# A retention-and-GLU kernel on one core: another order of first loads, split first gates, a ring of output rows, an earlier third pair

## The chip, the cores and the metric

The kernel runs on one core of a Trainium2 chip. A core has TensorE (PE, matrix products, with a separate weight-load step shown as PEld), VectorE (DVE), ScalarE (ACT), GpSimd (POOL) and SyncE (SP), each with its own instruction queue run in order, and 16 DMA engines that the queues feed. The metric is device time in microseconds, from the first to the last work of one execution. The kernel before took 339.49 us (median of six runs, 338.7 to 341.69).

## The reference

```python
scores = scale * np.matmul(q, k.transpose(0, 1, 3, 2))       # (8, 8, 576, 576), head size 64
gamma = 1.0 - 2.0 ** (-5.0 - np.arange(H))
Dmat = np.where(rel >= 0, gamma[:, None, None] ** rel, 0.0)    # rel = row - column
attn = np.matmul(scores * Dmat, v)                             # causal, decaying, no softmax
x = attn.transpose(0, 2, 1, 3).reshape(4608, 512)
gate = 1.0 / (1.0 + np.exp(-(x @ w_gate)))                     # 512 -> 1536
out = (gate * (x @ w_val)) @ w_out                             # 1536 -> 512, float32
```

Batch 8, 8 heads, 576 tokens, so 4608 rows for the gated layer. Inputs and output are float32; products run in bf16.

## The kernel before

**Retention by state.** The decay factors into a row factor on q and a column factor on k, so the first casts from float32 to bf16 multiply by small tables (L237 and L247/L257). Attention then needs only scores inside a chunk (masked), times v, plus q times a state: the running sum of k-transposed-v of all earlier chunks of that batch. The state sits in one PSUM bank (`st`), and each chunk copies it into a block-diagonal bf16 tile `sbd`, which the next chunk multiplies by its q. That is the state chain: state matmuls, copy, `inter` matmuls, next chunk.

**Three pairs, then 34 steps.** The first work is three "pairs" of two 128-token chunks each (batch 0 tokens 0-255 and 256-511, batch 1 tokens 0-255). A pair is cast (`cast_pair`, L234/L237), its k and q are transposed on PE (`turn`, L306, copied out by ACT at L316), scored (`pair_qk`, L325, masked by DVE at L330), multiplied by v (`pair_intra`, L365), joined with the state (`pair_st` L340, `tile_sv` L351, `pair_inter` L374) and written into `xT`, the transposed input of the gated layer (`pair_out`, L381/L384). All later chunks are "steps": POOL casts k, q and v (L247, L257, L268), a DMA transpose on SP turns them (`cross`, L284), and PE scores (L394), multiplies (L413, L415) and updates the state (L427).

**The gated layer.** `h` products take a 128-wide chunk of the 1536 (12 chunks) by a block of tokens: gate product, sigmoid on ACT, value product, multiplication on DVE into `gv`. `op` products (L557) multiply twelve `gv` by the out weights, 128 rows at a time; ACT copies the result into `ob` (L528) and SP stores it (L536). Tokens 0 to 511 come first and apart: gates in `h_both` (L606, sigmoid L610, product L613), out products in `op_first` (L733), with the third pair's work placed by hand between the out products. Then blocks of 256, 256, 4 x 384 and 4 x 512 tokens run through `h_units` (L490) and `op_units` (L557), and between their pieces the steps are advanced in proportion to the columns done.

**What sets the order.** The program's text: every engine runs its instructions in the order written, and semaphores between engines follow from which tile each one reads and writes. All loads, stores and DMA transposes but one store go through SP's queue, in the order written, and eight DMAs at most are under way. Loads use a ring of 18 buffers of 256 KB (`ld_pool`): pair 0, pair 1 (each k, q, k, q, v, v, by halves of the heads), gate and value weights, the twelve out weights, then pair 2, then steps. PSUM has eight banks: `tr`, two `qk`, `pv`, `st` and three `ffn`; a new tile of a name waits until the bank's last reader is done. `fill(n)` issues n matmuls of a blank tile that nobody reads, in places where PE would wait. Weight casts are dealt by hand to POOL, ACT and DVE. `store` holds each output row tile for two pieces of work before its DMA is written into SP's order (`tick`); rows of tokens before 768 wait until the block at 768.

## Time and profile before

| | |
|---|---|
| median of six runs | 339.49 us |
| the profiled execution | 338.84 us |
| its span, first to last instruction | 337.1 us |
| PE busy | 327.5 us (97%) |
| POOL, ACT, DVE busy | 185.4, 168.3, 163.6 us |
| DMA | 60.0 MB, 178 GB/s on average |
| first gate product of the gated layer | 19.65 us |
| first out product | 40.84 us |
| first product of the 512-token block (256 tokens) | 56.67 us |

The page of the profile is one execution. In the views by time a row has its start, how long it ran from its first start to its last end, engine, line, operation, output and input, how many instructions, and in brackets the engine's idle time ahead of it and what ended it. PE's matmuls overlap in the pipeline, so a row's length is a little more than the sum of the steps between starts. The granted clock of PE is 1.00 up to 331 us.

### The profile page before, as it was taken

What the parts mean: (1) busy time and instruction counts of PE and PEld (TensorE: products, weight loads), DVE (VectorE), ACT (ScalarE), POOL (GpSimd) and SP (SyncE); (2) the same over time, 40 slices, a digit from 0 to 9 for tenths busy, and PEclk for the clock granted to TensorE, in tenths of its full rate; (3) what the DMA queues carried; (4) which work ended last, traced back from release to release, by engine and by line L of the source; (5) the groups of instructions that cost most, each with busy time, mean ns of one, the idle gap of its engine ahead of it and who ended that gap; (6) DMA issues with size and microseconds to landing.
All of it is one profiled execution on the core that took longest, in us unless ns stands there. A gap on an engine that the chain in (4) does not pass through costs nothing.

```text
span 337.1 us, 7347 instructions
## 1 busy us (share of the span) xinstructions
PE 327.5 (97%) x2749; PEld 184.5 (55%) x2784; DVE 163.6 (49%) x327; ACT 168.3 (50%) x346; POOL 185.4 (55%) x327
## 2 busy tenths in 40 slices
PE   8899999999999999999999999999999999999996
PEld 4544445869666466556556655544555455444443
DVE  5744564726466455526446635642664156503320
ACT  6545535637665456355446655445545455233321
POOL 5574579788955979697548976482567500000000
PEclk9999999999999999999999999999999999999999
DMA  7999994899999999999969999892994440020002
GB/s 208 313 368 387 348 231 87 142 229 194 204 234 264 190 202 222 230 245 220 197 146 202 182 232 214 158 216 96 195 223 80 140 65 3 0 94 33 0 31 95
DMA packets 164100, 60.00 MB, mean 178 GB/s; under 512 B 144480, under 2 KB 156000, under 8 KB 164064
## 3 DMA queue, kind: packets, MB, share of 16 engines
q1 hardware_dynamic: 163920, 59.39, 85.5%
q8 instruction: 22, 0.36, 0.5%
q10 hardware_dynamic: 144, 0.13, 0.1%
q14 instruction: 14, 0.11, 0.1%
HBM read 37.75 MB, written 9.44 MB: 140 GB/s over the span
## 4 chain that ended last, share of the span: by engine, by line
PE 84%; DMA 7%; POOL 4%; issue 1%; DVE 1%; SPq 1%; ACT 0%; POOLq 0%; DVEq 0%
PE h L490 45%; PE op L557 23%; PE hg L606 3%; DMA T<-qk_nat 3%; PE hv L606 3%; PE qk L394 2%; PE pv L415 2%; DMA k32p<-in_k_dram 2%; PE pv L413 2%; DMA v32p<-in_v_dram 2%; PE st L427 2%; POOL qk_nat L247 1%; SPq L114 1%; PE op L547 1%; POOL qk_nat L257 1%
## 5 line engine op out<-in xcount | busy, mean ns | idle before, releaser
L490 PE MATMUL h<-xT,wg_sb 128*128 128x384 bf16 (+2 forms) x476 | 102.4, 336 | 0.4 <-DVE gv L518 0.2
L490 PE MATMUL h<-xT,wv_sb 128*128 128x384 bf16 (+2 forms) x473 | 102.2, 336 | 0.4
L247 POOL TENSOR_TENSOR qk_nat<-k,ktab 64x256 bf16<-64x256 f32 x120 | 73.5, 612 | 47.4 <-PE st L427 25.0
L518 DVE TENSOR_TENSOR gv<-g,h 128x384 bf16<-128x384 bf16 (+1 forms) x96 | 59.7, 622 | 71.7 <-PE h L490 56.7
L557 PE MATMUL op<-wo_sb,gv 128*128 128x512 bf16 x356 | 84.5, 379 | 0.8
L514 ACT ACTIVATE g<-h 128x384 bf16<-128x384 f32 (+1 forms) x96 | 52.2, 544 | 64.9 <-PE h L490 58.3
L433 DVE CAST sbd<-st 64x256 bf16<-64x256 f32 x104 | 43.7, 420 | 45.1 <-PE st L427 42.9
L490 PEld LDWEIGHTS <-wg_sb 128*128 128x128 bf16 x480 | 43.7, 98 | 31.4 <-issue 0.4
L490 PEld LDWEIGHTS <-wv_sb 128*128 128x128 bf16 x480 | 44.1, 98 | 29.0 <-issue 0.4
L557 PEld LDWEIGHTS <-gv 128*128 128x128 bf16 x372 | 34.4, 98 | 36.3
L268 POOL CAST vbd<-v 64x256 bf16<-64x256 f32 x120 | 47.6, 397 | 10.6 <-PE pv L415 6.1
L278 ACT CAST vs<-v 64x256 bf16<-64x256 f32 x104 | 41.9, 403 | 1.6
L528 ACT COPY ob<-op 128x512 f32<-128x512 f32 x34 | 19.8, 586 | 45.4 <-PE op L557 39.4
L257 POOL TENSOR_TENSOR qk_nat<-q,qtab 128x512 bf16<-128x512 f32 (+1 forms) x34 | 35.4, 1042 | 2.6
L417 ACT CAST xT<-pv 128x512 bf16<-128x512 f32 (+1 forms) x34 | 18.2, 534 | 18.1 <-PE pv L415 18.0
L396 DVE TENSOR_TENSOR pt<-qk,tri 128x512 bf16<-128x512 f32 (+1 forms) x34 | 21.2, 625 | 6.5 <-PE qk L394 6.2
L415 PE MATMUL pv<-pt,vbd 128*128 128x64 bf16 x240 | 18.0, 193 | 0.0
L427 PEld LDWEIGHTS <-qk_nat 128*128 128x128 bf16 x208 | 13.2, 98 | 8.8
L413 PE MATMUL pv<-T,sbd 128*128 128x64 bf16 x216 | 17.1, 193 | 0.0
L415 PEld LDWEIGHTS <-vbd 128*128 128x128 bf16 x240 | 15.2, 98 | 3.5
L413 PEld LDWEIGHTS <-sbd 128*128 128x128 bf16 x216 | 15.1, 98 | 2.5
L506 DVE TENSOR_TENSOR gv<-g,h 128x256 bf16<-128x256 bf16 x24 | 10.0, 421 | 12.2 <-ACT g L504 11.8
(76 smaller groups left out, 232.0 us busy)
## 6 DMA issues: line engine op xcount, KB each, us to landing
out_dram<-ob SPq DMA_DIRECT2D x34, 256.0 KB, 2.4
v<-in_v_dram SPq DMA_DIRECT2D x26, 256.0 KB, 4.2
k<-in_k_dram SPq DMA_DIRECT2D x26, 256.0 KB, 4.5
q<-in_q_dram SPq DMA_DIRECT2D x26, 256.0 KB, 5.1
wg<-in_moe_w_gate_dram SPq DMA_DIRECT2D x12, 256.0 KB, 5.7
wv<-in_moe_w_val_dram SPq DMA_DIRECT2D x12, 256.0 KB, 5.4
wo<-in_moe_w_out_dram SPq DMA_DIRECT2D x12, 256.0 KB, 5.3
k32p<-in_k_dram SPq DMA_DIRECT2D x6, 256.0 KB, 5.5
```

Source lines behind the costliest of these rows:

```text
L247: nc.gpsimd.tensor_tensor(out=kn[half(hh), j, :, half(hh)], in0=k32[half(j), hh::2, :], in1=ktab[half(j), c, hh::2].unsqueeze(2).to_broadc ...
L257: nc.gpsimd.tensor_tensor(out=qs[0:n], in0=q32[0:n], in1=qtab[0:n, c, :].unsqueeze(2).to_broadcast([n, H, D]), op=ALU.mult)
L268: nc.gpsimd.tensor_copy(out=vb[half(hh), j, :, half(hh)], in_=v32[half(j), hh::2, :])
L278: nc.scalar.copy(out=natural["vs", s][half(hh), j], in_=loaded[s][0][half(j), hh::2, :])
L396: nc.vector.tensor_tensor(out=pt[:, :, 0:n].rearrange("p m (j t) -> p m j t", t=64), in0=qkp[:, :, 0:n].rearrange("p m (j t) -> p m j t", ...
L413: nc.tensor.matmul(pvp[:, m, half(j)], lhsT=before[:, m, :], rhs=qT[:, m, half(j)], start=True, stop=False)
L415: nc.tensor.matmul(pvp[:, m, half(j)], lhsT=vb[:, j, m, :], rhs=pt[:, m, half(j)], start=before is None, stop=True)
L433: nc.vector.tensor_copy(out=sb[half(hh), :, half(hh)], in_=st_tiles[b][half(hh)])
L490: nc.tensor.matmul(out, lhsT=w_sb[:, kc, fc * P:(fc + 1) * P], rhs=xT[:, kc, t0 + a:t0 + e], start=(kc == 0), stop=(kc == NKC - 1))
L514: nc.scalar.activation(out=g[:, 0:n], in_=h1[:, 0:n], func=AF.Sigmoid)
L518: nc.vector.tensor_tensor(out=gvs[some[0]][:, a:e], in0=g[:, 0:n], in1=h2[:, 0:n], op=ALU.mult)
L557: nc.tensor.matmul(opp, lhsT=gvs[fc][:, nb * P:(nb + 1) * P], rhs=wo_sb[:, fc, :], start=(fc == 0), stop=(fc == NFC - 1))
```

## The change

Four edits, all in the order of work; nothing that is computed changes.

1. **Loads and the front.** k and q of pair 0 and pair 1 are loaded first (eight loads), then v of both (four). The front is written anew: casts of all k, then all v, then the first weights on POOL; scores of both pairs ahead of most v products; transposes in the banks `tr` and `pv`. Fillers go from 28 to 21, all into one tile.
2. **Gates of 256 tokens.** The first two chunks are computed by `h_half` on columns 0 to 255 and 256 to 511 apart, gate and value halves in one PSUM tile; the groups of columns 0 to 255 stand between the last state and `inter` steps of pair 1.
3. **The third pair.** Its k and q are loaded behind two out weights and its v behind six more; its transposes stand among the value products of chunks 8 to 11, its scores right behind them; two clears of `vbd` on POOL move ahead of the out weights.
4. **Ring of output rows.** A stored row tile's DMA is written when nine younger ones are held; the rest leave in the last two blocks.

```diff
             parts[nm, "pair", A, g] = t
+            yield
...
-    load_pair(0)
-    load_pair(1)
+    both = [load_pair(A) for A in range(2)]
+    for n_pair in (4, 2):
+        for one in both:
+            for _ in range(n_pair):
+                next(one)
     load_w(0, 2)
...
     load_w(8, 4)
-    for f in range(NFC):
-        load_wo(f)
-    load_pair(2)
+    pair_2 = load_pair(2)
+    for n_wo, n_pair in ((2, 4), (6, 2), (4, 0)):
+        for _ in range(n_wo):
+            load_wo(sum(1 for x in parts if x[0] == "o"))
+        for _ in range(n_pair):
+            next(pair_2)
     LEAD_CAST = 3
...
+    idle = ffn_psum.tile([P, 512], FP32, tag="ffn", name="idle")
     def fill(n):
...
-        ps = ffn_psum.tile([P, 512], FP32, tag="ffn", name=f"idle_{fill.at}")
-        fill.at += 1
         for i in range(n):
-            nc.tensor.matmul(ps, lhsT=blank[:, 0:P], rhs=blank, start=True, stop=True)
-    fill.at = 0
+            nc.tensor.matmul(idle, lhsT=blank[:, 0:P], rhs=blank, start=True, stop=True)
     fill(10)
...
         if g == 0:
-            probs["p", A] = att_pool.tile([P, 2, M, 2, P], BF16, tag="ptp", name=f"ptp_{A}", bufs=1)
+            probs["p", A] = att_pool.tile([P, 2, M, 2, P], BF16, tag="ptp", name=f"ptp_{A}", bufs=2)
         for hh in range(2):
...
+    def pair_tile(A, a, banks):
+        s = 2 * A + a
+        ps = [psum.tile([P, M // len(banks), P], FP32, tag=tag, name=f"pvp_{s}_{i}") for i, (psum, tag) in enumerate(banks)]
+        pair_ps[s] = [(ps[m * len(banks) // M], m % (M // len(banks)), M // len(banks)) for m in range(M)]
     def pair_intra(A, g, a):
         s = 2 * A + a
-        if g == 0:
-            pair_ps[s] = (tr_psum if a else pv_psum).tile([P, M, P], FP32, tag="tr" if a else "pv", name=f"pvp_{s}")
-        ps = pair_ps[s]
+        if s not in pair_ps:
+            pair_tile(A, a, [(tr_psum, "tr") if a else (pv_psum, "pv")])
         for i in range(2):
             m = 2 * g + i
+            ps, at_m, of = pair_ps[s][m]
             for r in range(2):
                 for hh in range(2):
-                    nc.tensor.matmul(ps[half(hh), m, :], lhsT=natural["v", A][half(a), r, 2 * m + hh, :],
+                    nc.tensor.matmul(ps[half(hh), at_m, :], lhsT=natural["v", A][half(a), r, 2 * m + hh, :],
                                      rhs=probs["p", A][half(a), hh, m, r, :],
-                                     start=(m == 0 and r == 0), stop=(m == M - 1 and r == 1),
+                                     start=(at_m == 0 and r == 0), stop=(at_m == of - 1 and r == 1),
                                      skip_group_check=True)
...
         for m in range(M):
-            nc.tensor.matmul(pair_ps[2 * A + a][:, m, :], lhsT=state[b, c - 1, 1][:, m, :],
+            ps, at_m, of = pair_ps[2 * A + a][m]
+            nc.tensor.matmul(ps[:, at_m, :], lhsT=state[b, c - 1, 1][:, m, :],
                              rhs=turned["qp", A][:, m, a * P:(a + 1) * P],
-                             start=False, stop=(m == M - 1), skip_group_check=True)
-    def pair_out(A, a, eng):
+                             start=False, stop=(at_m == of - 1), skip_group_check=True)
+    def pair_out(A, a, *engs):
         t0 = (2 * A + a) * P
-        if eng is not None:
-            eng(out=xT[:, :, t0:t0 + P], in_=pair_ps[2 * A + a])
-            return
-        for g, half_eng in enumerate((on_dve, on_act)):
-            half_eng(out=xT[:, 2 * g:2 * g + 2, t0:t0 + P], in_=pair_ps[2 * A + a][:, 2 * g:2 * g + 2])
+        k = M // len(engs)
+        for i, eng in enumerate(engs):
+            eng(out=xT[:, i * k:(i + 1) * k, t0:t0 + P], in_=pair_ps[2 * A + a][i * k][0])
...
-    LATE = 768
+    KEEP = 9
     stores = []
...
-    def store(opp, r0, hold, eng=None):
+    def leave():
+        r, ob = stores.pop(0)
+        for p0, r0, w in rows(r, P):
+            nc.sync.dma_start(out[r0:r0 + w, :], ob[p0:p0 + w])
+    def store(opp, r0, eng=None):
...
         (eng or on_act)(out=ob, in_=opp)
-        stores.append([hold if r0 >= LATE else 10 ** 6, r0, ob])
-    def tick(n=1):
-        for x in list(stores):
-            x[0] -= n
-            if x[0] <= 0:
-                for p0, r0, w in rows(x[1], P):
-                    nc.sync.dma_start(out[r0:r0 + w, :], x[2][p0:p0 + w])
-                stores.remove(x)
+        stores.append((r0, ob))
+        if len(stores) > KEEP:
+            leave()
...
                     yield 4 * 512
-            store(opp, t0 + nb * P, 2)
+            store(opp, t0 + nb * P)
             yield 4 * 512
...
         for _ in units:
-            tick()
+            pass
...
-    cast_pair("k", 0, 0, nc.gpsimd)
+    for A in range(2):
+        for g in range(2):
+            cast_pair("k", A, g, nc.gpsimd)
+    for A in range(2):
+        for g in range(2):
+            cast_pair("v", A, g, on_pool)
+    for i in range(2):
+        cast_w("g", 0, 2, i, on_pool)
+    for i in range(2):
+        cast_w("v", 0, 2, i, on_pool)
+    QK = [(qk_psum, "qk"), (qk_psum, "qk")]
+    FF = [(ffn_psum, "ffn"), (ffn_psum, "ffn")]
+    TR, PV = (tr_psum, "tr"), (pv_psum, "pv")
     cast_pair("q", 0, 0, nc.vector)
-    cast_pair("k", 0, 1, nc.gpsimd)
+    turn("k", 0, 0, *TR)
+    turn("q", 0, 0, *PV)
+    fill(3)
     cast_pair("q", 0, 1, nc.vector)
-    cast_pair("v", 0, 0, on_pool)
-    cast_pair("v", 0, 1, on_pool)
-    cast_pair("k", 1, 0, nc.gpsimd)
-    cast_pair("k", 1, 1, nc.gpsimd)
-    cast_pair("v", 1, 0, on_pool)
-    cast_pair("v", 1, 1, on_pool)
-    QK = [(qk_psum, "qk"), (qk_psum, "qk")]
-    turn("k", 0, 0)
-    turn("q", 0, 0)
-    fill(4)
-    turn("k", 0, 1)
     pair_qk(0, 0, QK)
-    turn("q", 0, 1)
+    turn("k", 0, 1, *TR)
+    fill(2)
+    turn("q", 0, 1, *PV)
     fill(3)
-    pair_qk(0, 1, QK)
+    cast_pair("q", 1, 0, nc.vector)
+    pair_qk(0, 1, FF)
+    turn("k", 1, 0, *TR)
+    turn("q", 1, 0, *PV)
+    fill(2)
+    cast_pair("q", 1, 1, nc.vector)
+    turn("k", 1, 1, *TR)
+    pair_qk(1, 0, QK)
+    fill(1)
+    turn("q", 1, 1)
     pair_intra(0, 0, 0)
...
     tile_sv(0, 0, (on_act, on_act))
-    cast_pair("q", 1, 0, nc.vector)
-    cast_pair("q", 1, 1, nc.vector)
-    fill(2)
-    turn("k", 1, 0)
     pair_intra(0, 1, 0)
+    pair_qk(1, 1, FF)
     pair_intra(0, 1, 1)
-    fill(2)
+    pair_st(0, 1)
     pair_inter(0, 1)
-    turn("q", 1, 0)
     pair_out(0, 0, on_act)
-    pair_st(0, 1)
-    fill(1)
-    turn("k", 1, 1)
     pair_out(0, 1, on_dve)
-    turn("q", 1, 1)
-    pair_qk(1, 0, QK)
     tile_sv(0, 1, (on_act, on_act))
-    fill(3)
-    pair_qk(1, 1, QK)
-    fill(1)
     pair_intra(1, 0, 0)
-    pair_inter(1, 0)
+    pair_tile(1, 1, QK)
     pair_intra(1, 0, 1)
+    pair_intra(1, 1, 0)
     pair_st(1, 0)
     tile_sv(1, 0, (on_act, on_act))
-    fill(2)
-    pair_intra(1, 1, 0)
-    pair_out(1, 0, on_act)
+    pair_inter(1, 0)
+    pair_out(1, 0, on_dve)
     pair_intra(1, 1, 1)
+    hp = {}
+    first_g = {}
+    def h_half(what, fc, x):
+        w_sb, i = (wg_sb, 0) if what == "g" else (wv_sb, 1)
+        if what == "g":
+            hp[fc, x] = ffn_psum.tile([P, 2, 256], FP32, tag="ffn", name=f"h_0_{x}_{fc}")
+        if x == 0 and what == "g":
+            first_g[fc] = g_pool.tile([P, 512], BF16, tag="g", name=f"g_0_{fc}")
+            gvs[fc] = gv_pool.tile([P, 512], BF16, tag="gv", name=f"gv_0_{fc}")
+        cols = slice(x * 256, x * 256 + 256)
+        for kc in range(NKC):
+            nc.tensor.matmul(hp[fc, x][:, i, :], lhsT=w_sb[:, kc, fc * P:(fc + 1) * P], rhs=xT[:, kc, cols],
+                             start=(kc == 0), stop=(kc == NKC - 1))
+        if what == "g":
+            nc.scalar.activation(out=first_g[fc][:, cols], in_=hp[fc, x][:, 0, :], func=AF.Sigmoid)
+        else:
+            nc.vector.tensor_tensor(out=gvs[fc][:, cols], in0=first_g[fc][:, cols], in1=hp[fc, x][:, 1, :], op=ALU.mult)
+    h_half("g", 0, 0)
     pair_inter(1, 1)
-    pair_out(1, 1, None)
-    for i in range(2):
-        cast_w("g", 0, 2, i, on_pool)
-    cast_w("v", 0, 2, 0, on_pool)
-    cast_w("v", 0, 2, 1, on_dve)
-    units = h_both((0, 1))
-    step(units, 1)
+    pair_out(1, 1, on_dve, on_act)
+    h_half("g", 1, 0)
     pair_st(1, 1)
     tile_sv(1, 1, (on_act, on_act))
-    step(units, 3)
+    h_half("v", 0, 0)
+    h_half("v", 1, 0)
+    for fc in range(2):
+        h_half("g", fc, 1)
+        h_half("v", fc, 1)
     for i in range(2):
...
     cast_w("v", 8, 4, 3, on_dve)
-    units = h_both((8, 9, 10, 11))
-    step(units, 2)
+    for t in vbd[0:2]:
+        nc.gpsimd.memset(t, 0.0)
     cast_wo(0, on_pool)
-    cast_wo(1, on_dve)
-    cast_wo(2, on_pool)
-    step(units, 2)
-    for f in range(3, 7):
-        cast_wo(f, on_pool if f % 2 else on_act)
-    step(units, 4)
-    for f in range(7, NFC):
-        cast_wo(f, on_pool if f % 2 else on_act)
     cast_pair("k", 2, 0, nc.gpsimd)
     cast_pair("k", 2, 1, nc.gpsimd)
+    cast_wo(1, on_dve)
+    cast_pair("q", 2, 0, nc.vector)
+    cast_pair("q", 2, 1, nc.vector)
+    units = h_both((8, 9, 10, 11))
+    step(units, 4)
+    cast_wo(2, on_pool)
+    turn("k", 2, 0, tr_psum, "tr")
+    step(units, 1)
+    cast_wo(3, on_act)
+    turn("q", 2, 0, pv_psum, "pv")
+    step(units, 1)
+    cast_wo(4, on_pool)
+    turn("k", 2, 1, tr_psum, "tr")
+    step(units, 1)
+    turn("q", 2, 1, pv_psum, "pv")
+    step(units, 1)
+    cast_wo(5, on_act)
+    cast_wo(6, on_pool)
+    cast_wo(7, on_pool)
     cast_pair("v", 2, 0, on_pool)
     cast_pair("v", 2, 1, on_pool)
-    cast_pair("q", 2, 0, nc.vector)
-    cast_pair("q", 2, 1, nc.vector)
-    nc.vector.memset(qk_nat[0], 0.0)
-    nc.vector.memset(qk_nat[1], 0.0)
-    later_constants()
-    for t in vbd[0:2]:
-        nc.gpsimd.memset(t, 0.0)
+    cast_wo(8, on_act)
+    cast_wo(9, on_pool)
+    cast_wo(10, on_act)
+    cast_wo(11, on_pool)
     loads_to(1)
...
     opps = [ffn_psum.tile([P, 512], FP32, tag="ffn", name=f"op_0_{nb}") for nb in range(3)]
-    op_first((0,), range(3), opps)
-    turn("k", 2, 0, tr_psum, "tr")
-    op_first((1,), range(3), opps)
-    turn("q", 2, 0, qk_psum, "qk")
-    op_first((2,), range(3), opps)
-    turn("k", 2, 1, pv_psum, "pv")
-    turn("q", 2, 1, qk_psum, "qk")
-    op_first((3, 4), range(3), opps)
     pair_qk(2, 0, QK)
-    op_first((5, 6), range(3), opps)
+    op_first((0, 1, 2), (0,), opps)
     pair_qk(2, 1, [(tr_psum, "tr"), (pv_psum, "pv")])
-    op_first((7,), range(3), opps)
+    nc.vector.memset(qk_nat[0], 0.0)
+    nc.vector.memset(qk_nat[1], 0.0)
+    op_first((0, 1, 2), (1, 2), opps)
+    later_constants()
+    op_first((3, 4, 5), range(3), opps)
     pair_st(2, 0)
     tile_sv(2, 0, (on_act, on_act))
-    cast_dense(0, 0)
-    cast_dense(0, 1)
-    op_first((8, 9, 10, 11), range(3), opps)
+    op_first((6,), range(3), opps)
     pair_intra(2, 0, 0)
...
     pair_out(2, 0, on_act)
-    store(opps[0], 0, 1, on_dve)
-    opps.append(ffn_psum.tile([P, 512], FP32, tag="ffn", name="op_0_3"))
-    op_first(range(0, 4), (3,), opps)
+    op_first((7,), range(3), opps)
     pair_intra(2, 1, 1)
...
     pair_out(2, 1, on_dve)
-    store(opps[1], P, 2, on_act)
-    op_first(range(4, 8), (3,), opps)
     pair_st(2, 1)
     tile_sv(2, 1, (on_dve, on_act))
-    store(opps[2], 2 * P, 3, on_act)
-    op_first(range(8, NFC), (3,), opps)
-    store(opps[3], 3 * P, 4, on_act)
+    cast_dense(0, 0)
+    cast_dense(0, 1)
+    op_first((8, 9, 10, 11), range(3), opps)
+    store(opps[0], 0, on_dve)
+    opps.append(ffn_psum.tile([P, 512], FP32, tag="ffn", name="op_0_3"))
+    op_first(range(0, 6), (3,), opps)
+    store(opps[1], P, on_act)
+    op_first(range(6, NFC), (3,), opps)
+    store(opps[2], 2 * P, on_dve)
+    store(opps[3], 3 * P, on_act)
     for t in vbd[2:4]:
...
     BLOCKS += [(t, 512) for t in range(2560, NT, 512)]
+    pieces = 0
     for w, (t0, n) in enumerate(BLOCKS):
...
         begin = at
-        if t0 == LATE:
-            for i, x in enumerate(stores):
-                x[0] = 4 + 3 * i
         total = 2 * NFC * 4 * n + 12 * 512 * (n // P)
...
         for cols in ffn_units(t0, n):
-            tick()
             gone += cols
+            pieces += 1
+            if stores and (nxt is None or w + 2 == len(BLOCKS) and pieces % 4 == 0):
+                leave()
             advance(begin + min(todo, -(-todo * gone // (total - 3 * 2048))))
         advance(end)
-    tick(100)
+    while stores:
+        leave()
...
```

## The prediction

> **What bounds the kernel now.** First the page's head, its engine table and the chain of waits by engine:
>
> ```profile
> span 337.1 us, 7347 instructions
> PE 327.5 (97%) x2749; PEld 184.5 (55%) x2784; DVE 163.6 (49%) x327; ACT 168.3 (50%) x346; POOL 185.4 (55%) x327
> ...
> PE 84%; DMA 7%; POOL 4%; issue 1%; DVE 1%; SPq 1%; ACT 0%; POOLq 0%; DVEq 0%
> ```
>
> TensorE carries the chain. The 97% also counts filler matmuls (L154) that compute nothing, so the second view is busy time by stage:
>
> ```profile
> 15.00:19.65 4.65, 3.45 (x76) 1.96 (x77) 2.73 (x6) 2.33 (x7) 2.75 (x5) 1.00 1.09 351
> 19.65:40.80 21.15, 21.05 (x110) 9.61 (x113) 10.71 (x17) 11.74 (x22) 11.85 (x20) 1.00 1.06 374
> 40.80:57.00 16.20, 15.12 (x166) 7.33 (x168) 8.57 (x14) 6.57 (x14) 13.31 (x22) 1.00 0.80 169
> 57.00:100.00 43.00, 42.78 (x456) 32.08 (x456) 24.51 (x57) 25.94 (x62) 33.67 (x60) 1.00 1.11 200
> ```
>
> The second column is PE's busy time. From 57 us on nothing is left between matmuls, and that work is the same in both kernels. Time can change only (1) before the first gates at 19.65, (2) between there and the 512-token block at 56.67, (3) in single waits after it. Third view, PE in order of time:
>
> ```profile
> 1.25 4.45 PE L154 MATMUL idle<-blank 128*128 128x512 bf16 x10 [1.25 <-DVE blank L147]
> ...
> 19.65 1.02 PE L606 MATMUL hg<-xT,wg_sb 128*128 128x512 bf16 x4 [0.61 <-DVE xT L384]
> ...
> 23.57 1.89 PE L606 MATMUL hg<-xT,wg_sb 128*128 128x512 bf16 x8
> ...
> 40.84 0.59 PE L733 MATMUL op<-wo_sb,gv 128*128 128x512 bf16 x2
> 41.85 0.38 PE L733 MATMUL op<-wo_sb,gv 128*128 128x512 bf16 x1 [0.42 <-DVE gv L613]
> 42.47 0.40 PE L306 MATMUL kTp<-ident,kp 128*128 128x128 bf16 x4 [0.24 <-POOL kp L237]
> ...
> 44.27 0.40 PE L306 MATMUL kTp<-ident,kp 128*128 128x128 bf16 x4
> 44.82 0.40 PE L306 MATMUL qTp<-ident,qp 128*128 128x128 bf16 x4
> ...
> 56.67 0.60 PE L490 MATMUL h<-xT,wg_sb 128*128 128x256 bf16 x4
> ```
>
> A 512-column matmul starts 0.216 after the one before it (eight in 1.73), one of 256 columns 0.109, a transpose 0.055. The holes are the steps beyond that: 0.58 before 41.85, 0.41 before 42.47, 0.33 before 44.82. Fourth, when POOL's casts start and what they waited for:
>
> ```profile
> 15.59 0.62 POOL L234 CAST vp<-v32p 128x512 bf16<-128x512 f32 x1 [1.28 <-DMA v32p<-in_v_dram]
> 16.35 1.37 POOL L214 CAST wg_sb<-wg 128x512 bf16<-128x512 f32 x2
> 17.85 0.62 POOL L214 CAST wv_sb<-wv 128x512 bf16<-128x512 f32 x1
> 19.37 1.37 POOL L214 CAST wg_sb<-wg 128x512 bf16<-128x512 f32 x2 [0.90 <-DMA wg<-in_moe_w_gate_dram]
> ...
> 50.99 2.66 POOL L247 TENSOR_TENSOR qk_nat<-k,ktab 64x256 bf16<-64x256 f32 x4
> ```
>
> Last, the one dense-stage wait for a DMA transpose and the SP queue ahead of it:
>
> ```profile
> 99.90 3.30 SPq L536 DMA_DIRECT2D out_dram<-ob  x5
> ...
> 106.83 3.10 SPq L284 DMA_TRANSPOSE T<-qk_nat  x1
> ```
>
> ```profile
> 111.95 0.41 PE L394 MATMUL qk<-T 128*128 128x64 bf16 x8 [0.24 <-DMA T<-qk_nat]
> ```
>
> **The change part by part.** The sum is against the profiled execution: 338.84 (span 337.1 and 1.7 around it), 0.65 below the median of 339.49.
>
> *Front: loads and order.* The twelve pair loads are the same size, in another order, on one queue, so the twelfth lands when it did: the last v cast still starts at 15.59 and ends at 16.21, the gate weights at 17.72. The second value-weight cast moves from DVE (0.84, at 19.42) behind the first on POOL: 17.85 + 0.62 + 0.62 gives 19.1. POOL's next cast waited 0.90 for its DMA, which covers the 0.62 put ahead of it. What is earlier is k and q of pair two (about 1.8, two slots of 0.9), so their scores are done before v is there. What PE has left once that v is cast, at 16.26: eight intra matmuls (0.18), 16 state matmuls (0.37), four inter (0.22), eight intra (0.18), and about 0.1 at each of four switches between half and whole array: 17.6. The first gate group (0.43, its second half after 17.72) and four inter end at 18.2, the second gate group and 16 state matmuls with two switches at 19.2, where the value weights are just ready (19.1). Two value groups: 20.1. Then gates and values of columns 256 to 511, four groups: 1.75. The instruction order of the changed kernel puts a wait for ACT on the first matmul of both these value groups: gate and value share one PSUM tile there, and nothing stands between them. Price: 0.16 from a gate group's last slot to its end, 0.38 for a 256-column sigmoid (ACT L504), and two hand-overs of 0.05: 0.64 each (a group's four starts span 0.44 of its 0.60, which gives the 0.16), bounds 0 and 0.86 (with the 0.60 of a 512-column sigmoid); I take 0.64, the row of this shape, twice. So hg of chunk 2 starts at 20.1 + 1.75 + 1.3 = 23.15, against 23.57: **-0.4** (bounds -1.7 without these waits, +0.1 at their high price). The 256-column halves cost 32 x 0.109 against 16 x 0.216, nothing. Two sigmoids of 0.60 become four of 0.38, two products of 0.69 four of 0.42: hidden, ACT and DVE are busy half of the stage; without that cover 0.3 each. The seven fillers fewer (28 to 21, 0.216 each) stood in waits and give nothing by themselves.
>
> For that shared tile the Trainium skill, "PSUM — Partial Sum Buffer", section "PSUM bank collisions raise a hardware error", says that two engines may not touch one bank at once and must be guarded by semaphore; by it the wait is no accident of the order. The trace of before shows no such case.
>
> *Third pair among the out weights.* Out weights land 0.68 apart, pair loads 0.9. Behind out weight 1 (33.7) k, q, k, q land at 34.6, 35.5, 36.4 and 37.3, out weights 2 and 3 at 38.0 and 38.7, the last at 45.9 as before. PE: hg of chunk 2 to 11 and hv to 7 is 16 groups of 0.864, so the first transpose stands at 23.15 + 13.8 = 37.0, when its k is cast. On ACT the cast of out weight 3 (38.7 to 39.25) stands ahead of the copy of q's first half (0.74, to 40.0); q's second transpose needs that bank, and PE comes to it at 40.3: cover of 0.3, beyond it one for one. On DVE the q casts stand ahead of the products of chunks 8 to 11 and end at 38.0, when hv of chunk 8 ends. The two memsets of vbd (1.84) move ahead of out weight 0's cast on POOL, into its wait for weights; no out weight is multiplied before 41. So the holes of 0.58, 0.41 and 0.33 go (1.3). One comes: the fourth accumulator takes the first one's bank, after DVE's copy (0.69, L528), with two matmuls behind the first's last: 0.38 + 0.69 + 0.1 - 3 x 0.216 = 0.52. Net -0.8; **-0.65** taken for the thin cover (bounds -0.8 and +0.2, when ACT is 0.7 late).
>
> *Waits for the transposes.* POOL's chain to the first step's k cast ends on the last load (45.87 either way); with v cast and two memsets already done it starts that cast 1.84 earlier, at 49.1. PE is 1.05 earlier, so the hole of 0.27 before the score group at 65.96 goes. The ring keeps nine rows, so no store is on SP until the tenth; the five stores ahead of the T issued at 106.83 are gone, and with them the hole of 0.41 before 111.95. **-0.65** of 0.68 (bounds 0 and -0.9).
>
> *Ring, tail.* Stores deferred: nine of 256 KB, landing in the last two blocks, where the queue is nearly empty (27 GB/s from 300 to 320 us). The last is still the ACT half-row copied at 333.85: 0, bounds -0.1 (the SP store of 333.42 no longer lies before it) and +0.5 (a store in its way).
>
> Sum -0.4 - 0.65 - 0.65 = **-1.7**: 337.1 for this execution, **337.8** beside the median.
>
> **The rivals.** *Front gates hidden* (B): weights come when they come (17.7, 19.1), the bank waits cost 0.86 each, and the transposes' waits turn up elsewhere: only the second part is left, 338.8. For it: DMA share 1.09 in the front. Against: the POOL row at 50.99, late by two memsets that are moved.
> *Bank waits free* (C): the value halves start at once: 1.3 more, 336.5. For it: gate and value groups of one 256-token chunk run back to back at L490. Against it: there the sigmoid follows both, here the wait stands between.
> *Slower: half clock* (D). Ten fillers at the start take 0.43 each, twice 0.216: PE starts at half rate until about 5.5. With seven fillers fewer, it could fall back while v is awaited (13 to 17 us). Price: the 7 us from 16.2 to 23.2 at half rate, of which about 5 are PE work: +5 - 1.7 = +3.3, 342.8; 1.7 us of PE work at half rate take the gain away, 3.4 make it slower by 0.5%. Against: before stayed at full rate with 3.45 of 4.65 us busy; after it I count some 9 of 12 us from 5.5 to 17.6, the same share, no hole above 0.7.
> The Trainium skill, "TensorE: Matmul & The Clock Gate", section "What's actually happening", puts the fall back after an idle window of about 3.4 us. By that rule D costs 0 and the sum stays; by the fillers alone it could cost 3.3.
>
> **How the numbers follow.** Forecast 0.66 (gain 1.0 to 2.4, half of it above 1.7), B 0.12, C 0.12, D 0.10. 0.5% is 1.7 us, about what a measurement tells from no change, and the forecast lies on it: faster 0.33 + 0.12 = 0.45, same 0.33 + 0.12 = 0.45, slower 0.10. The range takes in C with 0.5 of spread and B with 1.0: 336.0 to 339.8, D and the far ends left out; the forecast's own is 337.1 to 338.5.
>
> **What would show it.** hg of chunk 2 at 23.15 with two steps of 0.64 before value groups; the 512-token block at 55.6; L247's first cast at 49.1; no PE hole before L394. Wrong if those steps are missing (C), if PE waits for q's second transpose near 40, or if 512-column matmuls after 6 us start 0.43 apart (D).

## The result, and the profile after

| | before | after |
|---|---|---|
| median | 339.43 us (78 executions) | 338.55 us (38 executions) |
| lowest and highest | 337.89, 341.69 us | 336.73, 340.87 us |
| profiled execution, span | 338.84, 337.1 us | 337.30, 335.5 us |
| first gates of chunk 2 | 23.57 us | 23.63 us |
| 512-token block starts | 56.67 us | 55.86 us |

The ratio of the times is 0.9969, 95% interval 0.9957 to 0.9982: a gain of 0.3%, less than the 0.5% that the forecast took for about what a measurement can tell from no change. The profiles differ by 1.54 us, the medians by only 0.88. That gap has a cause of its own. Every execution's record holds the mean granted clock of TensorE. Of the 38 executions of the changed kernel 18 had 0.998 or more, and their median is 337.28 us; the other 20 had 0.988 to 0.995, and their median is 339.42. Of 65 executions of the kernel before that were taken beside the experiments, none is below 0.998. So the changed kernel is two things: 2.15 us faster than before (337.28 against 339.43) where the clock holds, and no faster where it doesn't. In the other kernels below the lost clock costs less: from 0.1 us (both_front, 338.24 against 338.14) to 1.4 (pair_as_before). The profiled execution of after is one where it holds; that of before was 0.6 below its median.

The page's engine table and chain, after (line numbers from here on are those of the changed kernel, some 10 to 60 higher than before):

```profile
PE 325.0 (97%) x2760; PEld 186.2 (55%) x2793; DVE 164.2 (49%) x330; ACT 167.9 (50%) x346; POOL 186.9 (56%) x328
...
PE 92%; SPq 2%; DMA 2%; issue 2%; ACT 1%; DVE 1%; POOL 0%
```

TensorE bounds it as before, and the DMA share of the chain went from 7% to 2%: the DMA transposes are off it, the first loads of v are still on it. New is 2% of "issue", time in which PE waited for nothing that the profile shows. PE in order of time, after, shows where:

```profile
15.68 0.41 PE L346 MATMUL st<-vp,kp 64*64 64x64 bf16 x14
17.35 0.22 PE L346 MATMUL st<-vp,kp 64*64 64x64 bf16 x2 [1.26 <-issue]
...
20.62 0.60 PE L698 MATMUL h<-xT,wg_sb 128*128 128x256 bf16 x4
21.69 0.60 PE L698 MATMUL h<-xT,wv_sb 128*128 128x256 bf16 x4 [0.47 <-ACT g L701]
...
23.20 0.60 PE L698 MATMUL h<-xT,wv_sb 128*128 128x256 bf16 x4 [0.47 <-ACT g L701]
23.63 1.89 PE L616 MATMUL hg<-xT,wg_sb 128*128 128x512 bf16 x7
...
40.70 0.39 PE L312 MATMUL qTp<-ident,qp 128*128 128x128 bf16 x4
...
53.27 2.75 PE L773 MATMUL op<-wo_sb,gv 128*128 128x512 bf16 x12 [0.35 <-DVE ob L544]
55.86 0.60 PE L501 MATMUL h<-xT,wg_sb 128*128 128x256 bf16 x4
...
57.72 0.40 PE L405 MATMUL qk<-T 128*128 128x64 bf16 x8
```

Sixteen state matmuls that belong together break after fourteen, and PE stands 1.26 us. Their operands had been there for the first fourteen. The two value groups wait as forecast: from the gate group at 20.62 to the value group at 21.69 are 1.07, of which 0.44 is work, so 0.64 each. From chunk 2's gates to the 512-token block it takes 32.23 us, before 33.10: the third pair's holes are gone, and the one forecast for the fourth accumulator (0.52 between starts) has come. From that block to the first matmul of the last row tile it is 273.54 (55.86 to 329.40) against 274.36: 0.82 less. The tail is the same 6.1 us in both.

When POOL's casts start, after:

```profile
14.31 0.62 POOL L240 CAST vp<-v32p 128x512 bf16<-128x512 f32 x1 [0.26 <-DMA v32p<-in_v_dram]
...
17.79 0.62 POOL L220 CAST wv_sb<-wv 128x512 bf16<-128x512 f32 x1 [0.64 <-DMA wv<-in_moe_w_val_dram]
...
49.48 2.66 POOL L253 TENSOR_TENSOR qk_nat<-k,ktab 64x256 bf16<-64x256 f32 x4
```

The last cast of v starts 1.28 earlier than before (15.59), the second value-weight cast ends at 18.41 and not at 19.1, and still the front ends no earlier: the stall is as long.

**A suspect for the stall.** The profile's table of DMA queues has one that no line of the kernel issues:

```profile
q8 instruction: 22, 0.36, 0.5%
```

These are 22 transfers of 16 KB. They keep step with PE's own instructions: in the steady part they start every 254 recorded matmuls and weight loads (some 3,300 records from the fetch at 98.23 us to the thirteenth after it). The transfer records place the first at 14.94 to 16.09 after, and at 13.16 to 14.36 before. Counting PE's instructions along the program, the break lies at number 448, the place where a new block of 256 would begin if some 64 stand ahead of the program; the block ahead of it begins at number 192. PE passed 192 at 10.21 and 448 at 17.43 before, 7.2 us apart. After, with the scores of both pairs done early and the work on v bunched behind its loads, it ran the same 256 instructions between 11.85 and 15.83, in 4.0 us.

### The profile page after: what moved, and what is told of

The parts are those of the page before. It is cut to its first block, busy times and chain, and to the rows that moved or that the text cites. A ratio compares the mean times of both kernels' runs of the same rounds, so it can differ in the third digit from the quotient of the medians.

```text
span 335.5 us, 7386 instructions
## 1 busy us (share of the span) xinstructions
PE 325.0 (97%) x2760; PEld 186.2 (55%) x2793; DVE 164.2 (49%) x330; ACT 167.9 (50%) x346; POOL 186.9 (56%) x328
## 4 chain that ended last, share of the span: by engine, by line
PE 92%; SPq 2%; DMA 2%; issue 2%; ACT 1%; DVE 1%; POOL 0%
PE h L501 48%; PE op L567 24%; PE op L773 3%; PE hv L616 3%; PE hg L616 3%; PE pv L426 2%; PE qk L405 2%; PE pv L424 2%; PE st L438 2%; SPq L114 2%; DMA v32p<-in_v_dram 2%; PE h L698 1%; PE op L557 1%; PE st L346 1%; PE pvp L377 1%
```

## The experiments

Two theories on the stall. *Instruction fetch*: PE reached the end of a block before the next one was there. *State group*: something about that group, its bank, ACT's copy or v. On the missing time in the median: *idle PE* against *one long stall* as what sets off the lower clock. On the parts: each edit undone alone, against the terms of the sum.

The table gives each kernel's ratio to before with its interval, the executions with a mean clock below 0.998, and the median of those at full clock less the median of before in the same measurement.

| kernel | ratio | below 0.998 | at full clock |
|---|---|---|---|
| after | 0.9969 (0.9957 to 0.9982) | 20 of 38 | -2.15 us |
| fetch_early | 0.9955 (0.9931 to 0.9978) | 2 of 9 | -1.82 |
| own_banks | 0.9940 (0.9922 to 0.9958) | 7 of 10 | -2.87 |
| both_front | 0.9959 (0.9943 to 0.9975) | 3 of 6 | -1.64 |
| fetch_shift_timed | 0.9908 (0.9882 to 0.9933) | 0 of 6 | -2.84 |
| front_as_before | 0.9935 (0.9916 to 0.9953) | 0 of 6 | -2.45 |
| idle_front | 0.9952 (0.9932 to 0.9973) | 9 of 12 | -2.44 |
| pair_as_before | 0.9989 (0.9969 to 1.0008) | 8 of 12 | -1.27 |
| ring_undone | 0.9984 (0.9961 to 1.0007) | 7 of 12 | -1.72 |
| clears_late | 0.9986 (0.9965 to 1.0007) | 6 of 10 | -1.47 |
| old_front_plus | 0.9901 (0.9876 to 0.9926) | 0 of 6 | -3.25 |
| new_front_plus | 0.9869 (0.9841 to 0.9897) | 1 of 6 | -4.32 |

**The stall moved in time: fetch_early.** The fillers are matmuls of a blank tile; cutting one into four keeps its time and adds six instructions.

```diff
-    fill(10)
+    fill(10, 4)      # 40 matmuls of 128 columns
...
-    fill(3)
+    fill(3, 4)
...
-    fill(2)
+    fill(2, 4)
...
-    fill(3)
+    fill(3, 4)
```

> The changed kernel with the same filler columns before the second scores cut into four times as many matmuls (18 of 512 columns become 72 of 128), so that PE's instruction count runs 108 ahead; nothing else. Theory 'instruction fetch': PE reads its instructions in blocks of 256, the DMA for a block is issued when PE enters the block ahead of it and is usable some 5.5 us later among the loads (entry at 11.85, PE free again at 17.35); the changed kernel ran the block between in 4.0 us (11.85 to 15.83), so PE stood 1.26. With the count 108 ahead the block is entered near 8.5 and the next one needed near 14.2, 5.7 later: the sixteen state matmuls at 15.68 run in one go, no issue wait of 1.26, and the gates of chunk 2 start at 22.4 instead of 23.63. Of these 1.25 the third pair gives part back: q's second transpose came at 40.70 and its bank is free at 40.07 (out weight 3's cast and a copy on ACT), a cover of 0.63. So the 512-token block starts at 55.2 and the span is 334.85 against 335.5; the ratio to before about 0.995. Rival 'the stall belongs to that state group' (its bank, ACT's copy or v): it stays at 1.26, chunk 2 at 23.6, span 335.5, ratio 0.997.

The stall went: the sixteen state matmuls run in one go, and no issue wait is left there. The span is 335.1, and the ratio 0.9955 as expected, but that is the clock's doing (2 of 9 below 0.998): at full clock the kernel is no faster than after, rather 0.3 slower by the table. Chunk 2 starts at 23.20, not at 22.4. The fetch now lies at 10.87 to 12.08, and the load that passed then came late:

```profile
13.55 0.61 POOL L240 CAST vp<-v32p 128x512 bf16<-128x512 f32 x1 [1.59 <-DMA v32p<-in_v_dram]
```

The trace notes a load's landing in sixteen parts. Fifteen parts of this one were there at 12.17 us and the last at 13.50, and the loads behind it kept that lag. In twelve of the fourteen profiles the last part falls 0.35 to 1.7 us further behind the fifteenth with the first fetch. A transfer of 16 KB takes 1.1 to 1.2 us there, and its share in the table fits one of the sixteen DMA engines; that the late part is the one on that engine is a reading, since the records don't name engines. So a fetch isn't free in this front; it costs less where the load that it meets has slack.

**The stall moved in the program: fetch_shift, fetch_shift_timed.**

```diff
-    fill(10)
+    fill(4, 4)
+    fill(6)
```

> The changed kernel with only the first four of the ten start fillers cut in four: PE's instruction count runs 24 ahead. Theory 'instruction fetch': the block is entered at 11.7 instead of 11.85, so the stall stays (1.3 to 1.6) but moves twelve matmuls forward in the program: the sixteen state matmuls near 15.6 break after two, not after fourteen. Rival 'the stall belongs to that state group': it breaks after fourteen as before, or not at all.

In this one execution neither came: no stall at all, chunk 2 at 22.41. The fetch had started at 12.68, 1.13 after PE passed number 192; in the changed kernel it was 3.09 after. So "5.5 us later" was wrong as a constant. Over all the profiles the fetch starts 1.1 to 3.8 us after PE passes that place, takes 1.1 to 1.2, and where PE stood it resumes 1.3 to 1.5 after its end (six profiles).

> The kernel of fetch_shift (four of the start fillers cut in four, PE's instruction count 24 ahead) again, now timed. Of the changed kernel's 38 executions 18 ran at full clock (median 337.28) and 20 had a mean clock of 0.988 to 0.995 (median 339.42); of 44 of the kernel before none was below 0.998. Theory 'the instruction stall sets off the half clock': without the stall (its one profile had none and chunk 2's gates at 22.41) all executions run at full clock, the median is about 0.3 under the changed kernel's 337.28 at full clock, ratio to before 0.993. Rival 'the front's order itself does it' (fewer fillers, v late): about half the executions below 0.998 again, ratio 0.996.

The median is 336.92, 0.9908, and all six executions are at full clock. This time the profile also shows the break, PE in order of time:

```profile
15.76 0.22 PE L347 MATMUL st<-vp,kp 64*64 64x64 bf16 x2
16.37 0.41 PE L347 MATMUL st<-vp,kp 64*64 64x64 bf16 x14 [0.39 <-issue]
```

The sixteen break after two, not after fourteen: twelve matmuls, which are 24 instructions, earlier in the program, exactly the shift. The fetch ended at 14.99, PE resumed at 16.37. The stall is 0.39 us long, and not 1.3 to 1.6 as expected: the fetch again started sooner after PE entered its block, 1.1 to 2.3 us in the five profiles with more fillers in the count and 3.0 to 3.8 in five without. Why isn't shown. The theory of the state group falls, that of the instruction fetch stands.

**The shared PSUM tile: own_banks.**

```diff
+            own = (tr_psum, "tr") if fc == 0 else (pv_psum, "pv")
+            hv_of[fc, x] = own[0].tile([P, 256], FP32, tag=own[1], name=f"hv_0_{x}_{fc}") if x else hp[fc, x][:, 1, :]
...
-            nc.tensor.matmul(hp[fc, x][:, i, :], lhsT=w_sb[:, kc, fc * P:(fc + 1) * P], rhs=xT[:, kc, cols],
+            nc.tensor.matmul(hv_of[fc, x] if i else hp[fc, x][:, 0, :], lhsT=w_sb[:, kc, fc * P:(fc + 1) * P], rhs=xT[:, kc, cols],
```

> The changed kernel with the value products of columns 256 to 511 of chunks 0 and 1 in PSUM tiles of their own (banks of the first pairs' products, free by then); nothing else. Theory 'shared tile': the two steps of 0.64 before the value groups go, chunk 2's gates start at 22.35 instead of 23.63; the issue wait of 1.26 near 16 us stays. From there as above: cover of 0.63 at q's second transpose, the 512-token block at 55.2, span 334.85, ratio to before about 0.995. Rival 'the sigmoid is waited for anyway' (gate and value in order on the engines): the steps stay, span 335.5, ratio 0.997.

PE in order of time:

```profile
17.64 0.22 PE L346 MATMUL st<-vp,kp 64*64 64x64 bf16 x2 [1.51 <-issue]
...
22.45 0.60 PE L702 MATMUL h<-xT,wg_sb 128*128 128x256 bf16 x4
22.88 0.60 PE L702 MATMUL hv<-xT,wv_sb 128*128 128x256 bf16 x4
```

Gate and value groups now start 0.44 apart: the 0.64 was the price of the shared tile. At full clock the kernel is 0.7 faster than after (three executions), as expected. The profile itself fell among the executions with a clock drop, and starts chunk 2 at 24.19.

**Both: both_front.** The two edits together.

> Both edits together: filler matmuls cut in four and value products in tiles of their own. Chunk 2's gates start at 21.1 (2.5 earlier). Theory 'the third pair takes it back': weights of chunks 4 to 7 are cast by 25.1, and the bank for q's second transpose is free at 40.07 whatever PE does, so the 512-token block still starts at 55.2 and the span is 334.85: no more than each edit alone, with a hole of about 1.9 at or ahead of q's second transpose. Rival 'the front is what counts': all 2.5 arrive, block at 53.4, span 333.0, ratio 0.990.

```profile
40.02 0.38 PE L312 MATMUL qTp<-ident,qp 128*128 128x128 bf16 x4 [0.42 <-ACT qT L322]
...
55.17 0.60 PE L501 MATMUL h<-xT,wg_sb 128*128 128x256 bf16 x4
...
58.63 0.41 PE L405 MATMUL qk<-T 128*128 128x64 bf16 x8 [1.43 <-DMA T<-qk_nat]
```

The block starts at 55.17, as the first theory said, though the front ended at 22.32 and not at 21.1 (v was late again, with a fetch at 10.86), and so the wait at q's transpose is 0.42 and not 1.9. What neither theory had: the first step's transpose is then late by 1.43. It took 5.5 us from issue to landing, with an instruction fetch at 56.08 to 57.02 inside it. In fetch_early, where a fetch covers its last 0.7 us, it took 4.2, and in the twelve profiles with no fetch inside it 3.8 to 3.9. The span is 336.4. A front that is faster by itself gave nothing.

**The clock: front_as_before, idle_front.** Load order, front and first gates of the kernel before, the rest as changed; then the same without the fillers between 13 and 18 us.

```diff
-    for n_pair in (4, 2):                              # front_as_before, with the old front's text
-        for one in both:
-            for _ in range(n_pair):
-                next(one)
+    for one in both:
+        for _ in range(6):
+            next(one)
```

> The changed kernel with the load order, the front and the first two chunks' gates of the kernel before; third pair, clears and ring as changed. Theory 'the front gained nothing' (chunk 2 at 23.63 against 23.57): chunk 2's gates at 23.6, the 512-token block at 55.8, span 335.5, ratio to before 0.997, and no issue wait over 0.5 on PE in the first 25 us (its instruction block is entered at 10.2 and the next needed at 17.4, 7.2 later). By the prediction on record the front is worth 0.4: span 335.9, ratio 0.998.

Chunk 2 at 23.53, the block at 55.76, span 335.4, median 337.27: with the old front the kernel is as fast as the changed one at full clock, and all six of its executions are at full clock. As changed, the new front gains nothing and puts the clock at risk. The last v cast comes early here too, with the load order of before, which had it at 15.59:

```profile
14.51 0.61 POOL L240 CAST vp<-v32p 128x512 bf16<-128x512 f32 x1 [0.21 <-DMA v32p<-in_v_dram]
```

```diff
-    fill(1)                                            # idle_front, against front_as_before
     turn("k", 1, 1)
...
-    fill(3)
     pair_qk(1, 1, QK)
-    fill(1)
     pair_intra(1, 0, 0)
...
-    fill(2)
     pair_intra(1, 1, 0)
```

> The kernel of front_as_before (front of the kernel before, no instruction stall, six of six executions at full clock) with the seven fillers between 13 and 18 us left out, so that PE idles about 1.5 us more there, in pieces under 1 us. Theory 'idle PE sets off the half clock, whatever it waits for': part of the executions fall below a mean clock of 0.998 and take about 2 us longer, median 338 to 339, ratio 0.995 to 0.998. Rival 'it takes one long stall': none falls, and the fillers gone win at most 0.4: median 337.0 to 337.3, ratio 0.992 to 0.9935.

Nine of twelve fell below 0.998, median 338.56. Busy time by stage of its profile (second column PE's busy time, then the other engines', and after them the granted clock):

```profile
3.90:17.60 13.70, 10.95 (x231) 6.71 (x230) 8.87 (x15) 8.38 (x17) 7.67 (x10) 1.00 1.12 304
17.60:24.40 6.80, 6.19 (x45) 2.38 (x34) 0.76 (x2) 3.07 (x7) 4.54 (x9) 0.50 1.06 373
24.40:40.00 15.60, 15.60 (x77) 7.23 (x76) 9.96 (x15) 7.41 (x14) 9.83 (x14) 1.00 1.08 358
```

PE ran at half clock from 17.6 to 24.4 us. There is no fetch stall in this profile, so idle PE is enough to set it off; the fillers that compute nothing were holding the clock. The longest hole before the drop is 1.05, about the "pieces under 1 us" that were meant, while the profiled executions of after and both_front kept the clock through 1.26 and 1.51. In the profiles of own_banks, clears_late and new_front_plus the drop lasts 3.4 us behind holes of 1.51, 1.63 and 1.10, here and in pair_as_before 6.8. These lengths make the mean clocks of 0.995 and 0.990 that most of the slower executions have: half of 3.4 us in 336 is 0.5%.

The clock records say what one hole doesn't. Each of the five drops starts three or four times 3.41 us after the clock's first rise to full (here 17.57 and 3.92), and that rise is at another time in each profile, from 3.92 to 7.30 us. Divide each profile from its rise on into stretches of 3.41 us. Three stretches at full clock have PE busy for under 0.6 of the time (0.52, 0.55 and 0.56, in clears_late, idle_front and own_banks), and all three end in a drop. Six have 0.65 to 0.68, and two of them do (pair_as_before, new_front_plus). None with more does, up to 325 us. So the idle time within such a stretch fits the drops better than any one hole: the 1.51 of both_front lay across the border of two (0.71 and 0.67). It would also explain why the drop is a draw: the same hole meets the stretches differently in each execution. A sharp limit isn't shown.

**The third pair, the ring, the clears, each undone.**

```diff
-    for n_wo, n_pair in ((2, 4), (6, 2), (4, 0)):     # pair_as_before: all out weights, then pair 2;
+    for f in range(NFC):                               # casts, transposes and out products in the old order
+        load_wo(f)
```

> The changed kernel with the third pair as before: loaded behind all out weights, its transposes among the out products, the clears late; front and ring as changed. Theory: the holes before its transposes come back (1.3) and the one of 0.52 before the fourth accumulator goes, so the 512-token block is at 56.7 instead of 55.86 (+0.87); the first step's k cast is late again at 51.0 and the hole of 0.27 before a score group near 66 is back; the ring keeps the later hole of 0.41 away. Span 335.5 + 0.87 + 0.3 = 336.65, ratio to before 0.9995. Rival 'the third pair's place is hidden by the last loads': block at 55.9, span 335.5.

At full clock it is 0.9 slower than after by the table (1.2 between the medians themselves): the size of the expectation. The kernel has the clears late too, and clears_late alone, below, costs 0.7 (1.0; four executions each), so the two gains don't add: at full clock little of the third pair's is left without the earlier clears. Its profile is no test of the holes, because the front there lost 3 us to a stall of 1.74 and the half clock, and with PE that late only the first hole of 0.58 was left.

```diff
-        if len(stores) > KEEP:
-            leave()
+        stores.append([hold if r0 >= LATE else 10 ** 6, r0, ob])     # ring_undone: tick() as before
```

> The changed kernel with the output rows stored as before (each held for two pieces of work, five early ones let go together at 768); front and third pair as changed. Theory: five stores stand again ahead of one DMA transpose on SP, and a hole before a score group near 111 is back: 0.41 as before, up to 1.2 since PE is 0.8 earlier there; 0.4 taken: span 335.9, ratio to before 0.998. Rival 'the ring does nothing': span 335.5, ratio 0.997, no hole over 0.2 near 111.

The chain's wait near 111, PE's waits from 100 to 115 us (total, times, longest):

```profile
PE qk L405 <- DMA T<-qk_nat: 2.0, 1, 2.0
```

The hole is back, at 2.0 and not at 0.41; the whole kernel is 0.4 slower than after at full clock by the table, as expected. At full clock the five executions run from 337.02 to 339.69, while front_as_before and fetch_shift_timed, which keep the ring, stay within 0.7 each. So this wait seems to differ between executions, and the profile of before had caught a small one; it was seen in these two profiles only.

```diff
-    for t in vbd[0:2]:
-        nc.gpsimd.memset(t, 0.0)
...
     cast_wo(11, on_pool)
+    for t in vbd[0:2]:                                 # clears_late
+        nc.gpsimd.memset(t, 0.0)
```

> The changed kernel with the two clears of vbd (1.84 us on POOL) behind the last out weight's cast, as before, and nothing else. Theory: the first step's k cast starts at 51.3 instead of 49.48, and PE, which comes 0.82 earlier than before to the first steps, waits for a transpose: 0.27 as before plus these 0.82, 1.1 in all near 58 to 66 us: span 336.6, ratio to before 0.9995. Rival 'the cast chain has slack': no hole over 0.3 there, span 335.5 to 335.8.

The first k cast is late as expected (51.08), and at full clock the kernel is 0.7 slower than after. No hole is seen in its profile, since PE itself was 1.8 late there (block at 57.66). The price holds in size; its place wasn't seen.

**Two better versions.**

```diff
-    opps.append(ffn_psum.tile([P, 512], FP32, tag="ffn", name="op_0_3"))
+    opps.append(qk_psum.tile([P, 512], FP32, tag="qk", name="op_0_3"))
...
-    for t in vbd[2:4]:
-        nc.gpsimd.memset(t, 0.0)
+    for t in vbd[2:4]:                                 # moved ahead of op_first((0, 1, 2), (1, 2), opps)
+        nc.vector.memset(t, 0.0)
```

> The kernel of front_as_before with the fourth out accumulator in a score bank (its hole of 0.52 goes) and the two later clears of vbd on DVE instead of POOL (the first step's k cast 1.8 earlier, so that its transpose is there for PE, which comes 0.5 earlier). Block of 512 tokens at 55.2 instead of 55.76, span 334.9 against 335.4, median 336.75, ratio to before 0.992. If the transpose of the first step is what PE then waits for: the hole of 0.5 comes back before the first scores near 57, ratio 0.9935.

Median 336.51, ratio 0.9901, all executions at full clock and within 0.5 us; the hole before the fourth accumulator is gone.

```diff
-    for n_wo, n_pair in ((2, 4), (6, 2), (4, 0)):      # new_front_plus, with the edits of fetch_shift,
+    for n_wo, n_pair in ((0, 4), (8, 2), (4, 0)):      # own_banks and old_front_plus, all clears on DVE
...
-    cast_wo(3, on_act)
     turn("q", 2, 0, pv_psum, "pv")
...
     turn("q", 2, 1, pv_psum, "pv")
+    cast_wo(3, on_act)
```

> The changed kernel with all that the runs have shown: four start fillers cut in four, value products of columns 256 to 511 in banks of their own, k and q of the third pair loaded ahead of all out weights and cast first, out weight 3's cast behind the transposes' copies on ACT, the vbd clears on DVE, the fourth out accumulator in a score bank. Front 21.15 instead of 23.63, no hole at q's second transpose: block of 512 tokens at about 53.3 (from 55.86: 2.5 less, and 0.5 for the accumulator, less up to 0.5 where chunk 4's gate weights are cast at 25.1), then a wait of up to 1 for the first step's transpose. Span 333.3 (332.9 to 334.3), ratio to before 0.988 if all executions keep the full clock, 0.991 if half of them lose 2 us.

Median 335.58, ratio 0.9869: the fastest of all, a little better than expected. One execution in six lost the clock, and it is the profiled one (span 335.0, after a wait of 1.10 for v); at full clock the median is 335.44. The expected 21.15 for the front was not seen: chunk 2 starts at 23.61 in that profile.

## Why the prediction was right, and where it was not

The number was 337.8, in 336.0 to 339.8; the median is 338.55, on the side of "no change". It is right as a time and only partly right in its reasons.

- **Front, -0.4: failed, +0.06.** The two bank waits of 0.64 are there to the hundredth. Two other steps failed. The last v cast, taken as fixed at 15.59, came at 14.31. 15.59 was one draw: in before fifteen of that load's sixteen parts had landed by 14.51 and the last at 15.54, with a fetch at 13.16 to 14.36. With the old load order again, in front_as_before, that cast starts at 14.51. The second is the row of PE work behind v ("17.6"): from that cast's end to the first gate group it is 1.39 in the forecast and 3.24 after (14.93 to 18.17). It summed matmuls and left out that PE had to fetch them: 1.26 is the stall. The other 0.6 is work that it undercounted, 24 v products ahead of the state matmuls where it had eight. The earlier v hid 1.28 of this, and chunk 2 is 0.5 later than the forecast's 23.15. front_as_before shows the same from the other side: nothing is lost without the new front.
- **Third pair, -0.65: -0.87**, just past the bound of -0.8. The three holes of 1.3 went and 0.52 came; the "thin cover" at q's second transpose held (no wait at 40.70). It was thin all the same: both_front used it up.
- **Waits for transposes, -0.65: -0.82** in the profile. Mechanism right, size off: the 0.41 near 111 was one draw of a wait that is 2.0 in ring_undone's profile. At full clock the whole change is worth 2.15 and not 1.7.
- **Tail 0: 0.**
- **Half clock (rival D, chance 0.10): wrong in chance and size.** It was looked for in the wait for v before 17 us, priced at 5 us of PE work, and held off by "no hole above 0.7". Its reading that PE starts at half rate until 5.5 is short: the clock record of before first rises at 6.45. The hole that the forecast couldn't see was 1.26 in the profile, 0.9 to 1.7 in four others with that front, and 20 of 38 executions lost the clock, at 2.1 each. The Trainium skill, "TensorE: Matmul & The Clock Gate", section "What's actually happening", was weighed as a reason to price D at 0; its windows of 3,413 ns agree with the drops of 3.4 and 6.8 us here, but the drops came behind holes of 1.1 to 1.7, with PE busy for 0.52 to 0.68 of the 3.4 us before them. The measurement decides: far less than an idle window is enough.
- **B and C:** C fell, the waits of 0.64 are there. Of B the front's zero came true by another cause; its waits "elsewhere" did not come, and the 512-token block is 0.81 earlier.

The median of 338.55 mixes 337.28 and 339.42. It lies nearer to B's 338.8 than to the forecast's 337.8, and though all of these lie within the range, that the median is within 0.8 us of the forecast is partly luck: a larger gain at full clock and a lost clock, which the forecast gave one chance in ten, made up for each other.

## What to carry to other kernels

Count PE's instructions, not only their time. Where 256 of them (128 or so small matmuls with their weight loads) run in some 4 us while the DMA queues are full, PE can stand: from the entry into the block ahead to the next one's use it takes 3.5 to 6.5 us, an estimate from the three pieces below (1.1 to 3.8, 1.1 to 1.2, 1.3 to 1.5). The remedy can be as cheap as shifting the count by a few blank matmuls. Fillers in the waits of a load-bound front are worth their place, because they hold the clock; look at the granted clock of every execution, not of the profiled one, before a median is explained. A wait seen once in a profile is one draw: a load's landing that a forecast builds on can be one too, and what removes a wait's cause may be worth more than the hole.

## What the runs showed of the hardware

- PE's instructions come in blocks of 16 KB, one per 254 recorded matmuls and weight loads, on a queue of their own. In the loaded front a fetch started 1.1 to 3.8 us after PE entered the block ahead and took 1.1 to 1.2; in six of fourteen profiles PE stood 0.4 to 1.7 us on "issue" and went on 1.3 to 1.5 us after the transfer's end. The Trainium skill, "Runtime: NRT & Kernel Launch", section "Instruction fetch mechanics", gives the same block and calls the cost of crossing it mostly hidden: true of the dense stage here (no wait of PE on "issue" from 56 to 331 us before and after), not of the front.
- A fetch went with a later landing of what was under way: a load's last part fell 0.35 to 1.7 us behind (twelve of fourteen profiles), a cast of v waited 1.44 and 1.59 for its DMA, the first step's transpose landed after 5.5 and 4.2 us in place of 3.8 to 3.9.
- In seven kernels with idle time in the front TensorE fell to half clock in 50 to 75% of the executions, against none of 65 and none of 6 in before and front_as_before. In the five profiles that show it, it lasts 3.4 or 6.8 us and follows a stretch of 3.41 us in which PE was busy for 0.52 to 0.68 of the time.
